# Linear attention and MLP on one Trainium2 core: w_out as whole rows, stepped weight loads, and a new order of the start

## Chip, cores and metric

The kernel runs on 1 core of one Trainium2 chip. The metric is device microseconds (us) of the run; the median of a kernel's runs is quoted. A profiled execution's own length is called its span. Ratios between kernels are the mean time of one kernel's runs over that of the other's of the same rounds, so they are not quite the ratio of the medians quoted beside them; brackets hold the 95% interval. A verdict of faster or slower asks for 2%: by that rule the changed kernel and a_v2 below are slower, a_packed, a_tiles, b_rows and a_best are unclear, and the rest are the same as before; where a smaller difference is called a gain or a loss, its interval excludes 1.

In the lines of the profile PE is TensorE and PEld its weight loads, ACT ScalarE, DVE VectorE, POOL GpSimd and SP the sync engine; a q marks an engine's sequencer, which issues DMAs, and L585 is a line of kernel.py. `ps` is a PSUM bank, `xT` the transposed x, `gT` the product that the second layer reads, `cosh` the cosine, `sp` the decay's logarithm but for its sign (the `f` line before it is the exponential that it needs), `vb` v in bf16, and `qkt` the transposed q and k. The granted clock is the share of TensorE's full clock that the profile shows as granted.

## The reference

Linear attention with a decay per channel (4 batches, 8 heads, 768 tokens, head size 48), and then an MLP on its 3072 tokens of 384 values:

```python
f = 1.0 / (1.0 + np.exp(-f_logit))
for t in range(S):
    state = f[:, :, t, :, None] * state + np.einsum('bhd,bhe->bhde', k[:, :, t], v[:, :, t])
    y[:, :, t] = np.einsum('bhd,bhde->bhe', q[:, :, t], state)
# ... x = y as (3072, 384)
h = x @ w_in              # 384 x 2048
g = h * np.cos(h)
return g @ w_out          # 2048 x 384
```

## The kernel before

Attention works on 24 chunks of 128 tokens. Each chunk loads f, k, q and v. The decay sums of f go through TensorE (L416, L419), the states and scores follow, and the chunk's y is transposed to x. The MLP takes units of 128 or 256 tokens: a first-layer matmul group fills one PSUM bank (`ph`), ScalarE takes its cosine, VectorE multiplies, and the second layer sums 16 products to a 128x384 tile.

A list scheduler in Python (`Plan`) puts every operation on an engine and in an order when the kernel is built, from estimated durations and a table of priorities. Each engine then runs its list strictly in order. The framework adds the semaphores: it makes the reader wait for the transfer that wrote what it reads.

```python
GATES = [1, 0, 0, 0, 2, 3, 2, 2]      # four w_in slices, four w_out slices: each issued after
                                      # the v of this chunk has been used
QUEUES = ["SAAA", "ASSA", "SSSS", ...]  # who issues f, k, q, v of a chunk: S sync, A ScalarE, P GpSimd
QK_DMA = [7, 10, 13, ...]             # chunks whose q, k are transposed by DMA instead of TensorE
X_DMA = [11, 13, 15, ...]             # the same for y

w_in_bf = cpool.tile([128, KM, d_ff], BF16, name="w_in_bf")       # one tile, written by four DMAs
w_in_v = [Val(ap=w_in_bf[:, :, i * 512:(i + 1) * 512]) for i in range(NW)]

def load_weights(part, i, prio):
    if part == 0:
        dst = w_in_v[i]
        src = moe_w_in.rearrange("(km p) f -> p km f", p=128)[:, :, i * 512:(i + 1) * 512]
    else:
        dst = w_out_v[i]
        src = moe_w_out.rearrange("(kf p) m -> p kf m", p=128)[:, i * 4:(i + 1) * 4, :]
    # ... nc.gpsimd.dma_start(out=dst.ap, in_=src), gated by GATES

# first layer, one PSUM bank:
def g1(e, j=j, ph=ph):
    for g in range(G):
        f0 = (j * G + g) * 128
        for m in range(KM):
            nc.tensor.matmul(ph.ap[:, g * T:(g + 1) * T],
                             lhsT=w_in_bf[:, m, f0:f0 + 128], rhs=x[:, m, :], start=..., stop=...)
# P.op(..., reads=xs + [w_in_v[j * G // 4]])  then cosine on ScalarE, product on VectorE

order = P.run()
with tc.manual_schedule():
    table = None
    for o in order:
        if o.table is not None:
            if o.table == "E" and table != "E":
                nc.scalar.preload_act_table_set("natural_log_exp_and_others")
            table = o.table
        o.fn(o.eng)
```

Of the kernel before, what the change touches and what calls it, by code (L numbers as in the profile page):

```python
# [96 lines left out]
class Plan:  # L97


    SEM = 70.0  # L100
    DMA = 1.092
    WAIT = {'PE': 0.0, 'POOL': 97, 'DVE': 154, 'ACT': 409}
    RING = 3500.0
# [37 lines left out]
    def run(self):  # L141
# [15 lines left out]
        while len(order) < n:  # L157
            picks, first = [], {}
            for o in ready:
# [18 lines left out]
                for e, cost in o.eng.items():  # L178
# [3 lines left out]
                    if o.dma and e == "SP":  # L182
                        s = max(s, ring[0] - self.RING)
# [66 lines left out]
def kernel(  # L250
# [12 lines left out]
    C = 128  # L263
# [10 lines left out]
    GROUPS = [1, 1, 1, 1, 1, 1, 2, 2, 2, 2, 1, 1, 3, 2, 3]  # L274
    UNITS = [128, 128, 128, 128, 256, 256, 256, 256, 128, 128, 256, 256, 256, 256, 128, 128]
    ATT = [-10.16, -8.17, -4.99, 0.11, 6.14, 3.09, 4.17, 1.33, 2.29, 1.86, 5.6, 0.47, 2.61, 2.34, -2.58, -2.8, -5.5, -1.05, -1.76, -4.41, -2.39, 0.76, 4.74, -4.25]
    DEC = [-0.66, -1.41, 2.39, -0.73, 3.32, 1.22, -3.35, 0.65, -0.34, -1.28, 0.8, 2.4, 1.16, 2.8, -2.87, -1.43, -4.69, -4.08, -1.68, -2.98, 3.95, -1.37, -1.73, -0.08]
    MM1 = [6.38, -2.33, 5.15, 0.82, -3.52, 2.06, 3.26, -6.82, -3.23, -5.74, -4.4, -6.91, -6.01, -9.31, -13.24, -5.93, -9.36, -13.7, -5.96, -13.1, -8.32, -22.13, -16.43, -24.95]
    MM2 = [8.02, 8.08, 14.32, 8.13, 9.49, 9.01, 11.35, 24.51, 13.52, 4.27, 10.31, 19.31, 13.3, 8.66, 22.93, -2.07, -3.64, 10.08, 13.04, -1.99, 17.19, -1.14, 7.0, 16.95]

    GATES = [1, 0, 0, 0, 2, 3, 2, 2]

    QUEUES = ["SAAA", "ASSA", "SSSS", "SSSS", "SSSS", "SSSS", "SSSS"]

    QK_DMA = [7, 10, 13, 14, 15, 17, 18, 19, 20, 21, 22, 23]
    X_DMA = [11, 13, 15, 18, 19, 20, 22, 23]
    FAST = 12
    GT_BUFS = {128: 4, 256: 4}
# [22 lines left out]
    nld = 6  # L311
# [4 lines left out]
    vbS = slots("vb", 4, [128, H, D])  # L316
    spS = slots("sp", 5, [128, H, 64], zero=272.0)
    bS = slots("b", 4, [128, H * D + NP], F32)
    biS = slots("bi", 3, [128, H * D], F32)
    qkS = slots("qk", 4, [128, 2 * NP * C], zero=470.0)  # L320
    qktS = slots("qkt", 4, [128, 2 * NP, C])
    amS = slots("am", 4, [128, 4, C])
    szS = slots("sz", 3, [128, NP, 2 * D], zero=200.0)
    yS = slots("y", 3, [128, d_model])
    stS = slots("st", 2, [128, NP, D], F32)
    x_sb = [cpool.tile([128, KM, TOK], BF16, name=f"xT_{i}") for i in range(NT)]
    gS = {T: slots(f"gT{T}", n, [128, KF, T]) for T, n in GT_BUFS.items()}
    coS = slots("cosh", 4, [128, TOK])
    otS = slots("ot", 4, [128, d_model], F32)
    base = banks("ps", 8)  # L330
    moe_cap = [5, 0]
    phS = Banks(base, "ph", 4, [moe_cap])
    poS = Banks(base, "po", 2, [moe_cap])
    paS = Banks(base, "pa", 2)
    miS = Banks(base, "mi", 4)
# [8 lines left out]
    P.op({"POOL": 1100.0}, masks, prio=-1.0)  # L344
# [11 lines left out]
# [3 lines that stand above are left out]
            src = moe_w_in.rearrange("(km p) f -> p km f", p=128)[:, :, i * 512:(i + 1) * 512]  # L359
        else:  # L360
            dst = w_out_v[i]
            src = moe_w_out.rearrange("(kf p) m -> p kf m", p=128)[:, i * 4:(i + 1) * 4, :]
        o = P.op({"POOL": 850.0}, lambda e, dst=dst, src=src: nc.gpsimd.dma_start(
            out=dst.ap, in_=src), writes=[dst], prio=prio, lat=2200.0, dma=2400.0 if part == 0 else 2200.0)
# [15 lines left out]
    def chunk_load(b, c, prio):  # L380
        vals = []
        for pool, src in ((fS, f_logit), (kS, k), (qS, q), (vS, v)):
# [6 lines left out]
                 writes=[t], prio=prio, lat=3000.0 if way == "P" else 2000.0, dma=980.0)  # L389
# [3 lines left out]
    def decay_group(chunks, g, prio):  # L393
# [18 lines left out]
        for (b, c, ld, sp) in outs:  # L412
# [10 lines left out]
            P.op({"PE": 365.0}, pe, reads=[sp], writes=[pc], prio=prio, lat=170.0)  # L423
# [202 lines left out]
    for g, size in enumerate(GROUPS):  # L626
# [3 lines left out]
        for j, item in enumerate(decay_group(grp, g, n + DEC[g])):  # L630
            attend(*item, prio=n + j + ATT[n + j])
            if n + j == 0:
                for i in range(NW):
                    load_weights(0, i, 0.2 + 0.1 * i)
# [46 lines left out]
```

## Time and profile before

| | before |
|---|---|
| median of 3 runs | 192.81 us (192.74 to 194.06) |
| span of the profiled run (its time was 194.2 us) | 192.4 us |
| PE busy | 170.5 us, 89% |
| work PE cannot avoid (counts times spacing) | 160 us |
| PE's loss: whole, and before 50 us | 32.7 and 24.8 us |

"Loss" is time in which PE does not do work that it must do: the span, or a stretch of it, less the sum of its matmuls, each at the spacing that it has in a packed run. It counts waits, and also matmuls that run at half rate. The prediction shows how the spacings were read.

For comparing with later kernels, two stretches. First PE in the timeline of the kernel before (start, duration, engine, line, operation, output and inputs, count):

```profile
19.63 1.46 PE L585 MATMUL ps<-xT,w_in_bf 128*128 128x128 bf16 x12
...
22.61 0.83 PE L585 MATMUL ps<-xT,w_in_bf 128*128 128x128 bf16 x12
```

The first group of twelve first-layer matmuls runs at 19.63, the second at 22.61. The first takes 1.46 us for twelve, the second 0.83: the same instructions, at half rate and at full rate. Then the weight loads of the first layer by themselves (shortest, median and longest in ns):

```profile
L585 PEld LDWEIGHTS <-w_in_bf x768: 95/98/152, 19.6 to 180.7; 128*128 128x128 bf16 x192
```

### The profile page before, as it was taken

How to read it: one execution, taken by the hardware profiler on the slowest of the kernel's cores; microseconds unless marked ns; L12 is line 12 of the kernel's file. 1: busy time of each engine (PE TensorE's matmuls, PEld its weight loads, DVE VectorE, ACT ScalarE, POOL GpSimd, SP SyncE). 2: the span in 40 equal slices, each digit the busy share in tenths (PEclk: the TensorE clock that was granted, in tenths of full speed). 3: DMA queues.
4: the chain of work that ended last, by engine and by line, in shares of the span. 5: the costliest groups of instructions: out<-in, count | busy, mean ns of one | idle time of the engine just before them, and what ended most of it. 6: DMA issues, size and time to landing. Idle time of an engine off the chain costs nothing.

```text
span 192.4 us, 5056 instructions
## 1 busy us (share of the span) xinstructions
PE 170.5 (89%) x1960; PEld 129.5 (67%) x1960; DVE 138.0 (72%) x259; ACT 137.4 (71%) x250; POOL 65.6 (34%) x105
## 2 busy tenths in 40 slices
PE   0056996879999999999999999999999999999992
PEld 0035786747679668767769887588686785788861
DVE  6057995667978999995988798269878369782900
ACT  0434788599289968998989769998369992473620
POOL 5250806240030076029167211598321491200000
PEclk9999997899999999999999999999999999999999
DMA  6999999998995999996399899799993383102022
GB/s 137 218 205 191 217 186 154 197 200 157 200 232 126 221 189 217 197 258 113 85 271 121 180 200 219 179 224 166 201 243 111 117 120 87 54 0 82 3 84 81
DMA packets 123032, 31.00 MB, mean 161 GB/s; under 512 B 116352, under 2 KB 123008, under 8 KB 123008
## 3 DMA queue, kind: packets, MB, share of 16 engines
q1 hardware_dynamic: 114096, 26.55, 68.9%
q0 software_dynamic: 3712, 3.15, 10.4%
q10 hardware_dynamic: 5200, 0.98, 3.1%
q8 instruction: 15, 0.25, 0.6%
q14 instruction: 9, 0.07, 0.1%
HBM read 25.17 MB, written 4.72 MB: 155 GB/s over the span
## 4 chain that ended last, share of the span: by engine, by line
PE 78%; DVE 8%; ACT 3%; issue 3%; ACTq 3%; DMA 2%; DVEq 0%
PE ps L585 33%; PE ps L606 29%; PE ps L489 4%; PE ps L470 3%; ACTq L388 3%; DVE qk L447 3%; PE ps L540 2%; DVE am L496 2%; PE ps L416 2%; PE ps L508 2%; DMA out_dram<-ot 2%; PE ps L561 1%; PE ps L543 1%; DVE st L523 1%; ACT L648 1%
## 5 line engine op out<-in xcount | busy, mean ns | idle before, releaser
L606 PE MATMUL ps<-w_out_bf,gT 128*128 128x384 bf16 x384 | 70.6, 326 | 0.0
L585 PE MATMUL ps<-xT,w_in_bf 128*128 128x128 bf16 (+1 forms) x768 | 69.5, 251 | 0.6 <-DVE xT L550 0.4
L596 DVE TENSOR_TENSOR gT<-ps,cosh 128x512 bf16<-128x512 f32 x96 | 60.5, 686 | 11.0 <-ACT cosh L592 10.7
L585 PEld LDWEIGHTS <-w_in_bf 128*128 128x128 bf16 x768 | 60.9, 100 | 6.6 <-issue 0.9
L592 ACT ACTIVATE cosh<-ps 128x512 bf16<-128x512 f32 x96 | 53.6, 604 | 9.5 <-PE ps L585 6.8
L606 PEld LDWEIGHTS <-gT 128*128 128x128 bf16 x384 | 34.5, 97 | 19.3
L496 DVE TENSOR_TENSOR am<-ps,umask 128x512 bf16<-128x512 f32 x48 | 31.2, 685 | 4.0 <-PE ps L489 3.6
L527 POOL TENSOR_TENSOR sz<-st,b 64x192 bf16<-64x192 f32 x32 | 16.1, 503 | 52.0 <-DVE st L523 39.0
L452 POOL CAST vb<-v 128x384 bf16<-128x384 f32 x24 | 13.0, 543 | 27.4 <-DMA v<-in_v_dram 16.6
L447 POOL TENSOR_TENSOR qk<-k,bi 128x384 bf16<-128x384 f32 x16 | 16.0, 1003 | 7.5 <-ACT bi L426 7.3
L615 ACT COPY ot<-ps 128x384 f32<-128x384 f32 x13 | 6.2, 484 | 15.5 <-PE ps L606 15.5
L447 POOL TENSOR_TENSOR qk<-q,b 128x384 bf16<-128x384 f32 x13 | 13.0, 1001 | 12.0 <-ACT b L426 8.7
L416 PE MATMUL ps<-sp,umask 128*128 128x384 bf16 x24 | 8.4, 349 | 9.5 <-ACT sp L404 9.4
L648 ACT ACT_TABLE_LOAD x9 | 11.5, 1283 | 7.1 <-issue 7.0
L550 ACT CAST y<-ps 128x384 bf16<-128x384 f32 x19 | 9.0, 482 | 10.4 <-PE ps L543 4.8
L426 ACT ACTIVATE b<-ps 128x388 f32<-128x388 f32 x24 | 11.9, 494 | 5.5 <-PE ps L419 4.3
L523 DVE TENSOR_TENSOR st<-ps,sz 64x192 f32<-64x192 f32 x32 | 11.3, 352 | 4.1 <-PE ps L508 3.2
L476 DVE COPY qkt<-ps 128x512 bf16<-128x512 bf16 x21 | 8.4, 420 | 7.7 <-PE ps L470 7.6
L470 PE MATMUL ps<-ident,qk 128*128 128x128 bf16 x96 | 9.3, 238 | 4.6 <-DVE qk L447 4.5
L447 DVE TENSOR_TENSOR qk<-q,b 128x384 bf16<-128x384 f32 x11 | 8.1, 740 | 7.1 <-ACT b L426 7.0
L404 ACT ACTIVATE sp<-f 128x384 bf16<-128x384 f32 x24 | 12.6, 523 | 0.7
L419 PEld LDWEIGHTS <-sp 128*128 128x128 bf16 x96 | 6.2, 100 | 10.1 <-issue 8.1
(38 smaller groups left out, 152.2 us busy)
## 6 DMA issues: line engine op xcount, KB each, us to landing
out_dram<-ot SPq DMA_DIRECT2D x24, 192.0 KB, 2.9
f<-in_f_logit_dram SPq DMA_DIRECT2D x23, 192.0 KB, 3.7
k<-in_k_dram SPq DMA_DIRECT2D x23, 192.0 KB, 4.0
q<-in_q_dram SPq DMA_DIRECT2D x23, 192.0 KB, 4.0
v<-in_v_dram SPq DMA_DIRECT2D x22, 192.0 KB, 3.9
w_in_bf<-in_moe_w_in_dram POOLq DMA_DIRECT2D x4, 384.0 KB, 7.8
w_out_bf<-in_moe_w_out_dram POOLq DMA_DIRECT2D x4, 384.0 KB, 7.0
v<-in_v_dram ACTq DMA_DIRECT2D x2, 192.0 KB, 6.5
```

Of the source, the lines that this page charges most:

```text
L404: nc.scalar.activation(out=sp.ap[:, :, 0:D], in_=f.ap, func=AF.Ln, bias=1.0)
L447: lambda e, src=src, w=w, dst=dst: E(e).tensor_mul(out=dst.ap, in0=src.ap, in1=w.ap[:, 0:H * D].rearrange("p (h d) -> p h d", d=D)),
L452: o = P.op({"POOL": 510.0}, lambda e: nc.gpsimd.tensor_copy(out=vf.ap, in_=v32.ap), reads=[v32], writes=[vf], prio=prio)
L470: nc.tensor.transpose(out=o[:, i, :], in_=qk.ap[:, j * C:(j + 1) * C], identity=ident)
L496: nc.vector.tensor_mul(out=am.ap, in0=pa.ap.rearrange("p (a n) -> p a n", n=C), in1=umask[:, None, :].broadcast_to([128, 4, C]))
L523: P.op({"DVE": 370.0}, lambda e, g=g, sg=sg: nc.vector.tensor_add(out=sg.ap, in0=psv(g), in1=block(S_in.ap, g)), reads=[ps, S_in], writes= ...
L527: o = P.op(cost, lambda e, g=g, srcap=srcap, out=out: E(e).tensor_mul(out=out.ap, in0=srcap(), in1=bt.ap[rows(g), H * D:, None].broadcast_ ...
L585: nc.tensor.matmul(ph.ap[:, g * T:(g + 1) * T], lhsT=w_in_bf[:, m, f0:f0 + 128], rhs=x[:, m, :], start=(g == 0 and m == 0), stop=(g == G - ...
L592: P.op({"ACT": 490.0}, lambda e, ph=ph, co=co: nc.scalar.activation(out=co.ap, in_=ph.ap, func=AF.Sin, bias=HALF_PI), reads=[ph], writes=[ ...
L596: P.op({"DVE": 605.0}, lambda e, ph=ph, co=co, gv=gv: nc.vector.tensor_mul(out=gv.ap, in0=ph.ap.rearrange("p (g t) -> p g t", t=T), in1=co ...
L606: nc.tensor.matmul(po.ap[:, 0:d_model], lhsT=gT.ap[:, j, i * 128:(i + 1) * 128], rhs=w_out_bf[:, j, :], start=(j == 0), stop=(j == KF - 1))
L648: nc.scalar.preload_act_table_set("natural_log_exp_and_others")
```

## The change

Its intent: read w_out from memory in longer pieces (four whole rows to a partition, 6 KB), begin the exponentials sooner, start w_out's loads sooner, take work from PE by DMA transposes, and give the scheduler more buffers and better constants. A row of w_out in a partition is now row 4p + j of its slice, so row p of the first layer's output must be the same one. Therefore the weight loads read w_in with a step of four columns. Core of the diff (the new priority tables, groups, costs and buffer counts are cut; so is a loop of dummy matmuls, which runs zero times):

```diff
-    UNITS = [128, 128, 128, 128, 256, 256, 256, 256, 128, 128, 256, 256, 256, 256, 128, 128]
+    UNITS = [128, 128, 128, 128, 256, 128, 128, 128, 128, 256, 128, 128, 256, 256, 128, 128, 256, 256]
-    GATES = [1, 0, 0, 0, 2, 3, 2, 2]
+    GATES = [1, 1, 0, 1, 1, 2, 2, 1]
-    QUEUES = ["SAAA", "ASSA", "SSSS", "SSSS", "SSSS", "SSSS", "SSSS"]
+    QUEUES = ["SAAP", "SSSS", "SSSA", "SSSS", "SSSS", "SSAA", "SSSS"]
-    QK_DMA = [7, 10, 13, 14, 15, 17, 18, 19, 20, 21, 22, 23]
-    X_DMA = [11, 13, 15, 18, 19, 20, 22, 23]
+    QK_DMA = [7, 10, 12, 13, 14, 15, 16, 17, 18, 19, 20, 21, 22, 23]
+    X_DMA = [7, 8, 11, 12, 13, 14, 16, 18, 19, 20, 21, 22, 23]
+    WARM = 0
-    gS = {T: slots(f"gT{T}", n, [128, KF, T]) for T, n in GT_BUFS.items()}
+    gS = slots("gT", BUFS["g"], [128, KF, 256])
...
-            src = moe_w_out.rearrange("(kf p) m -> p kf m", p=128)[:, i * 4:(i + 1) * 4, :]
+            src = moe_w_out[i * 512:(i + 1) * 512, :].rearrange("(p j) m -> p j m", j=4)
...
-                    f0 = (j * G + g) * 128
+                    s0, f0 = divmod(j * G + g, 4)
                     for m in range(KM):
                         nc.tensor.matmul(ph.ap[:, g * T:(g + 1) * T],
-                                         lhsT=w_in_bf[:, m, f0:f0 + 128], rhs=x[:, m, :],
+                                         lhsT=w_in_bf[:, m, s0 * 512 + f0:(s0 + 1) * 512:4],
+                                         rhs=x[:, m, :],
...
+                P.op({"ACT": 1300.0}, lambda e: nc.scalar.preload_act_table_set(
+                    "natural_log_exp_and_others"), prio=0.0)
...
-        table = None
+        table = "E"
```

More of the change, by code (lines that the diff above doesn't have):

```diff
@@ L97 @@
 class Plan:
-    SEM = 70.0
-    DMA = 1.092
-    WAIT = {'PE': 0.0, 'POOL': 97, 'DVE': 154, 'ACT': 409}
-    RING = 3500.0
+    SEM = 80.0
+    DMA = 1.074
+    WAIT = {'PE': 0.0, 'ACT': 441.0, 'DVE': 176.0, 'POOL': 368.0}
+    RING = 2600.0
     def __init__(self):
@@ L181, in run @@
                     s = max(at, free[e])
-                    if o.dma and e == "SP":
+                    if o.dma and e != "POOL":
                         s = max(s, ring[0] - self.RING)
@@ L271 @@
     NT = n_tokens // TOK
-    GROUPS = [1, 1, 1, 1, 1, 1, 2, 2, 2, 2, 1, 1, 3, 2, 3]
-    UNITS = [128, 128, 128, 128, 256, 256, 256, 256, 128, 128, 256, 256, 256, 256, 128, 128]
-    ATT = [-10.16, -8.17, -4.99, 0.11, 6.14, 3.09, 4.17, 1.33, 2.29, 1.86, 5.6, 0.47, 2.61, 2.34, -2.58, -2.8, -5.5, -1.05, -1.76, -4.41, -2.39, 0.76, 4.74, -4.25]
-    DEC = [-0.66, -1.41, 2.39, -0.73, 3.32, 1.22, -3.35, 0.65, -0.34, -1.28, 0.8, 2.4, 1.16, 2.8, -2.87, -1.43, -4.69, -4.08, -1.68, -2.98, 3.95, -1.37, -1.73, -0.08]
@@ L278 @@
-    MM1 = [6.38, -2.33, 5.15, 0.82, -3.52, 2.06, 3.26, -6.82, -3.23, -5.74, -4.4, -6.91, -6.01, -9.31, -13.24, -5.93, -9.36, -13.7, -5.96, -13.1, -8.32, -22.13, -16.43, -24.95]
-    MM2 = [8.02, 8.08, 14.32, 8.13, 9.49, 9.01, 11.35, 24.51, 13.52, 4.27, 10.31, 19.31, 13.3, 8.66, 22.93, -2.07, -3.64, 10.08, 13.04, -1.99, 17.19, -1.14, 7.0, 16.95]
-    GATES = [1, 0, 0, 0, 2, 3, 2, 2]
-    QUEUES = ["SAAA", "ASSA", "SSSS", "SSSS", "SSSS", "SSSS", "SSSS"]
-    QK_DMA = [7, 10, 13, 14, 15, 17, 18, 19, 20, 21, 22, 23]
@@ L286 @@
-    X_DMA = [11, 13, 15, 18, 19, 20, 22, 23]
-    FAST = 12
-    GT_BUFS = {128: 4, 256: 4}
+    GROUPS = [1, 1, 1, 1, 1, 1, 1, 1, 2, 2, 1, 1, 2, 3, 3, 1, 1]
+    UNITS = [128, 128, 128, 128, 256, 128, 128, 128, 128, 256, 128, 128, 256, 256, 128, 128, 256, 256]
+    ATT = [19.22, 11.51, -4.12, -47.95, -0.79, -26.21, 1.62, -77.63, -4.72, -35.67, 4.42, -7.77, -2.18, -5.67, -30.35, -11.85, -82.53, -43.97, -72.33, -27.9, 14.06, -10.62, -90.56, -29.09]
+    DEC = [0.76, -37.4, -9.67, 3.24, -28.16, -26.29, -29.09, -13.37, -2.77, -22.73, -5.51, -16.89, -9.11, -15.8, -5.52, -15.87, -14.6, -47.95, -13.31, -46.04, 12.51, -38.96, -48.3, 2.6]
@@ new lines @@
+    MM1 = [31.51, -33.43, 5.49, -61.55, -31.58, -28.33, -84.44, -57.9, -92.94, -33.48, -15.49, -110.01, -86.82, -88.64, -49.22, -3.19, -33.68, 38.91, -19.02, -27.86, -47.17, -40.28, -25.45, -2.63]
+    MM2 = [17.68, 38.21, -7.69, 15.13, 1.62, -48.95, 20.6, 14.96, 12.07, -1.71, 12.39, 6.86, 48.36, 89.6, 44.19, 59.19, 89.52, -38.97, 26.19, 0.43, -54.56, -74.55, -67.19, 15.11]
+    GATES = [1, 1, 0, 1, 1, 2, 2, 1]
+    QUEUES = ["SAAP", "SSSS", "SSSA", "SSSS", "SSSS", "SSAA", "SSSS"]
+    QK_DMA = [7, 10, 12, 13, 14, 15, 16, 17, 18, 19, 20, 21, 22, 23]
@@ L290 @@
+    X_DMA = [7, 8, 11, 12, 13, 14, 16, 18, 19, 20, 21, 22, 23]
+    FAST = 10
+    WARM = 0
+    BUFS = {"ld": 7, "vb": 6, "sp": 6, "b": 6, "bi": 4, "qk": 5, "qkt": 6, "am": 6, "sz": 4, "y": 4, "st": 2, "co": 5, "ot": 5, "g": 6}
+    CAPS = [6, 4, 3, 3, 3]
     cpool = ctx.enter_context(tc.tile_pool(name="const", bufs=1))
@@ L309, in banks @@
         return Slots([ppool.tile([128, 512], F32, name=f"{name}_{i}") for i in range(n)], name)
-    nld = 6
+    nld = BUFS["ld"]
     fS = slots("f", nld, [128, H, D], F32)
@@ L315 @@
     vS = slots("v", nld, [128, H, D], F32)
-    vbS = slots("vb", 4, [128, H, D])
-    spS = slots("sp", 5, [128, H, 64], zero=272.0)
-    bS = slots("b", 4, [128, H * D + NP], F32)
-    biS = slots("bi", 3, [128, H * D], F32)
-    qkS = slots("qk", 4, [128, 2 * NP * C], zero=470.0)
-    qktS = slots("qkt", 4, [128, 2 * NP, C])
-    amS = slots("am", 4, [128, 4, C])
-    szS = slots("sz", 3, [128, NP, 2 * D], zero=200.0)
-    yS = slots("y", 3, [128, d_model])
-    stS = slots("st", 2, [128, NP, D], F32)
+    vbS = slots("vb", BUFS["vb"], [128, H, D])
+    spS = slots("sp", BUFS["sp"], [128, H, 64], zero=272.0)
+    bS = slots("b", BUFS["b"], [128, H * D + NP], F32)
+    biS = slots("bi", BUFS["bi"], [128, H * D], F32)
+    qkS = slots("qk", BUFS["qk"], [128, 2 * NP * C], zero=470.0)
+    qktS = slots("qkt", BUFS["qkt"], [128, 2 * NP, C])
+    amS = slots("am", BUFS["am"], [128, 4, C])
+    szS = slots("sz", BUFS["sz"], [128, NP, 2 * D], zero=200.0)
+    yS = slots("y", BUFS["y"], [128, d_model])
+    stS = slots("st", BUFS["st"], [128, NP, D], F32)
     x_sb = [cpool.tile([128, KM, TOK], BF16, name=f"xT_{i}") for i in range(NT)]
-    gS = {T: slots(f"gT{T}", n, [128, KF, T]) for T, n in GT_BUFS.items()}
-    coS = slots("cosh", 4, [128, TOK])
-    otS = slots("ot", 4, [128, d_model], F32)
+    gS = slots("gT", BUFS["g"], [128, KF, 256])
+    coS = slots("cosh", BUFS["co"], [128, TOK])
+    otS = slots("ot", BUFS["ot"], [128, d_model], F32)
     base = banks("ps", 8)
-    moe_cap = [5, 0]
-    phS = Banks(base, "ph", 4, [moe_cap])
-    poS = Banks(base, "po", 2, [moe_cap])
-    paS = Banks(base, "pa", 2)
-    miS = Banks(base, "mi", 4)
+    moe_cap = [CAPS[0], 0]
+    phS = Banks(base, "ph", CAPS[1], [moe_cap])
+    poS = Banks(base, "po", CAPS[2], [moe_cap])
+    paS = Banks(base, "pa", CAPS[3])
+    miS = Banks(base, "mi", CAPS[4])
     w_in_bf = cpool.tile([128, KM, d_ff], BF16, name="w_in_bf")
@@ L343, in masks, with idle @@
         make_upper_triangular(nc, umask, val=1.0, diag=True)
-    P.op({"POOL": 1100.0}, masks, prio=-1.0)
+    mk = Val()
+    P.op({"POOL": 1100.0}, masks, writes=[mk], prio=-1.0)
+    warm = Val(phS)
+    for i in range(WARM):
+        def idle(e):
+            for _ in range(2):
+                nc.tensor.matmul(warm.ap[:, 0:128], lhsT=ident, rhs=ident, start=True, stop=True)
+        P.op({"PE": 220.0 if i < 16 else 112.0}, idle, reads=[mk], writes=[warm], prio=1e6)
     for pool, cost in zeroed:
@@ L361, in load_weights @@
             dst = w_out_v[i]
-            src = moe_w_out.rearrange("(kf p) m -> p kf m", p=128)[:, i * 4:(i + 1) * 4, :]
+            src = moe_w_out[i * 512:(i + 1) * 512, :].rearrange("(p j) m -> p j m", j=4)
         o = P.op({"POOL": 850.0}, lambda e, dst=dst, src=src: nc.gpsimd.dma_start(
-            out=dst.ap, in_=src), writes=[dst], prio=prio, lat=2200.0, dma=2400.0 if part == 0 else 2200.0)
+            out=dst.ap, in_=src), writes=[dst], prio=prio, lat=3000.0, dma=2350.0 if part == 0 else 2000.0)
         gate(o, GATES[part * NW + i])
@@ L388, in chunk_load @@
             P.op(eng, lambda e, t=t, ap=ap, dma=dma: dma.dma_start(out=t.ap, in_=ap),
-                 writes=[t], prio=prio, lat=3000.0 if way == "P" else 2000.0, dma=980.0)
+                 writes=[t], prio=prio, lat=3000.0 if way == "P" else 1250.0, dma=980.0)
             vals.append(t)
@@ L421, in pe @@
                                      rhs=umask[:, C - 1:C], start=False, stop=(p == NP - 1))
-            P.op({"PE": 365.0}, pe, reads=[sp], writes=[pc], prio=prio, lat=170.0)
+            P.op({"PE": 268.0}, pe, reads=[sp], writes=[pc], prio=prio, lat=170.0)
             def ex(e, pc=pc, o=bt, s=-1.0, n=H * D + NP):
@@ L480, in attend @@
             P.op({"SP": 1000.0}, lambda e: nc.sync.dma_start_transpose(out=qkt.ap, in_=qk.ap),
-                 reads=[qtd, ktd], writes=[qdt, kdt], prio=prio, lat=2000.0, dma=1400.0)
+                 reads=[qtd, ktd], writes=[qdt, kdt], prio=prio, lat=1250.0, dma=1400.0)
         pas, ams = [Val(paS), Val(paS)], [Val(amS), Val(amS)]
@@ L492, in pe @@
                                      start=(p == 0), stop=(p == NP - 1))
-        P.op({"PE": 330.0}, pe, reads=[kdt, qdt], writes=pas, prio=prio, lat=170.0)
+        P.op({"PE": 420.0}, pe, reads=[kdt, qdt], writes=pas, prio=prio, lat=170.0)
         for pa, am in zip(pas, ams):
@@ L567, in attend @@
             P.op({"SP": 700.0}, lambda e: nc.sync.dma_start_transpose(out=x.ap, in_=yt.ap),
-                 reads=[yt], writes=[x], prio=prio, lat=2000.0, dma=480.0)
+                 reads=[yt], writes=[x], prio=prio, lat=1250.0, dma=480.0)
     def moe(u, t0, T):
         n0 = t0 // C
-        xs, gT = xT[n0:(t0 + T) // C], Val(gS[T])
+        xs, gT = xT[n0:(t0 + T) // C], Val(gS)
         x = x_sb[t0 // TOK][:, :, t0 % TOK:t0 % TOK + T]
```

## The prediction

> **What bounds the kernel now.** I began with the page's slices: TensorE (PE) and the DMA engines side by side.
>
> ```profile
> PE   0056996879999999999999999999999999999992
> ...
> DMA  6999999998995999996399899799993383102022
> ```
>
> A slice is 4.8 us. From the eleventh on PE is full to the end; before it PE has holes, and the DMA row is full there. So there are two regimes. The table of windows shows their border (PE busy with its count of matmuls, then PEld, DVE, ACT, POOL, granted clock, mean DMA share, GB/s):
>
> ```profile
> 0.00:10.00 10.00, 0.56 (x5) 0.41 (x5) 2.96 (x8) 2.35 (x4) 4.53 (x15) 1.00 1.07 179
> 10.00:20.00 10.00, 6.36 (x65) 4.43 (x66) 6.90 (x16) 4.81 (x11) 3.00 (x6) 1.00 1.26 196
> 20.00:30.00 10.00, 8.13 (x142) 7.47 (x139) 9.74 (x18) 8.03 (x13) 4.31 (x7) 1.00 1.24 201
> 30.00:40.00 10.00, 8.85 (x107) 7.33 (x108) 6.17 (x13) 7.40 (x13) 3.33 (x6) 0.83 1.13 183
> 40.00:50.00 10.00, 8.79 (x103) 6.39 (x102) 7.37 (x13) 8.56 (x14) 2.79 (x4) 1.00 0.88 173
> 50.00:180.00 130.00, 129.00 (x1483) 98.03 (x1482) 102.52 (x191) 102.87 (x193) 47.60 (x70) 1.00 0.78 161
> ```
>
> Busy time alone flatters PE, since a matmul waiting for its neighbour's end counts as busy. For what PE must do I used its spacing in packed runs, which the chain that ended last shows near the end (start, duration, what):
>
> ```profile
> 165.76 5.24 PE ps L585 x48
> ...
> 175.65 5.36 PE ps L585 x96
> 181.01 7.82 PE ps L606 x48
> ```
>
> That is 109 ns for a first-layer matmul with 256 tokens, 55.8 ns with 128 tokens, 163 ns for a second-layer one (384 columns). With the counts of the groups: 384 x 0.109 = 41.9, 384 x 0.0558 = 21.4, 384 x 0.163 = 62.6. The attention's matmuls in the same way (transposes 56 ns, scores 42, state and output 42 and 25, decay sums about 0.27 us a chunk) make about 34. Sum 160 us; the span is 192.4. So **32 us are lost by PE**. Summing the same per-instruction costs in 10 us stretches: 25 us are lost before 50 us, 4 between 50 and 180, the rest in the tail (last PE work ends at 188.8, then a 0.48 us copy and the last output's landing). The middle is as good as done; only the first 50 us, the tail, or PE's own work can pay.
>
> The start of the chain says what the first 8 us are:
>
> ```profile
> 0.74 0.48 ACTq L388
> ...
> 1.25 0.74 ACTq L388
> ...
> 2.02 1.19 ACTq L388
> ...
> 3.24 1.65 ACTq L388
> ...
> 4.93 2.00 ACTq L388
> ...
> 6.96 0.09 ACT L648
> 7.04 1.21 issue
> 8.25 0.53 ACT f L401
> ```
>
> ScalarE (ACT) issues five loads, each slower than the last, then loads its table, then starts the first exponential at 8.25. In the trace the first f tile landed at 4.16 us, so **4 us of that wait are ACT's own**. After it the landings rule: single loads arrive 0.9 us apart up to 12.7 us, the four slices of w_in at 15.1, 17.5, 20.0 and 22.7, of w_out at 28.2, 31.0, 36.0 and 39.8, and the sixth chunk is in at 47.6. PE cannot do its first-layer work before 22.7, nor finish a second-layer tile before 39.8.
>
> **What the skill says.** (1) "DMA: Bandwidth & Descriptors", section "Issuing engines are not separate DMA queues": loads started by different engines share the same 16 DMA engines, and spreading them saves only issue time. The trace agrees with the sharing: whichever queue issued them, the loads land 0.9 us apart. But issue time is not small here: the fifth issue held ACT for 2.00 us. (2) The same page, "Specifications", gives 512 bytes as the least for full rate. The loads have rows of 192 bytes: 192 KB in 0.9 us is 0.22 MB/us. A w_in slice reads 2 KB rows, 0.79 MB in 2.5 us, 0.31 MB/us. w_out's rows are 1536 bytes already, so joining four to 6144 gains little. (3) "SBUF — State Buffer", section "SBUF: two separate sides", box on cachelines: two accesses to each 16-byte line are enough for full rate, so a step of up to 8 bf16 is called free by its list; the same text's two hits per line would mean 8 bytes, 4 bf16. (4) "TensorE: Matmul & The Clock Gate", section "Weight-path perf modes", lists column steps up to 1,024 as allowed for fast weight loads, "packed or strided". Nothing in the kernel before loads weights with a step, so no run yet shows (3) or (4).
>
> **The change part by part.**
>
> *w_out as four whole rows.* To match it, h's rows are permuted, and the first layer's weight loads read w_in with a step of four elements (8 bytes). The number of loads follows the units: 12 of 128 tokens and 6 of 256, against 8 and 8, so 18 x 48 = 864 for 768. If stepped loads stay hidden, first-layer PE time is 576 x 0.0558 + 288 x 0.109 = 63.5 us against 63.3: nothing. DMA: w_out now 7 us to landing, 4 x about 0.2 us saved at w_in's rate: under 1 us, in the start where DMA counts.
>
> *First table load and queues.* The order of instructions shows ACT issuing k and q of chunk 0, then the table load, then the exponential; f goes on the sync queue, v by GpSimd. ACT is free at 2.0, the table at 3.3, f lands at about 4.2. Chunk 0's exponential moves from 8.25 to about 4.3: **4 us on the chain's start**. But w_in ends the stretch, not chunk 0. Its first slice is issued after v of chunk 0 (about 8 us, as now), the other three after v of chunk 1 (9.9 to 12.4, now 9.6 to 13.9). Landings of about 14.5 to 22 against 15.1 to 22.7: **about 1 us**, plus 1 us because attention of chunks 0 to 2 is then already out of the way.
>
> *w_out earlier.* Two slices follow w_in at once, in place of loads for chunk 3. PE may begin second-layer work near 26 us, now 35.3. It is the same DMA work in another order, so I credit **1 us** for filling.
>
> *More DMA transposes.* 14 of qk for 12, 13 of x for 8. PE loses 2 x 8 transposes x 56 ns = 0.9 and 5 x 3 x 63 ns = 0.95: **1.8 us less PE work** where PE is full. DVE and ACT lose about nine evacuations of some 0.4 us, which is off the path. DMA gains about 5 us, where its share is 0.78.
>
> *One pool of gT, more buffers, bank caps 6/4/3/3/3.* Six tiles of 256 tokens take the room of the old two pools. A little of the 4 us lost in the middle: **0.3 us**. *No dummy matmuls*: the loop runs zero times and the kernel before had none: 0. Table loads stay 18 in all.
>
> Sum: 1 + 1 + 1 + 1.8 + 0.3 = 5.1 us less. I take off 0.3 for small new waits of a rearranged order: 192.8 - 4.8 = **188.0 us**.
>
> **The rivals.** *A: the step spoils the weight loads.* If a stepped load cannot hide behind a 128-token matmul and the pair takes the 100 ns that one load lasts in the trace, that is 576 x 44 ns = 25 us: about 213. Half that harm would be 200. For it: no measurement. Against it: 8 bytes still give two hits a line, and the author re-measured other PE costs in his plan but left this one. I give it 8%.
>
> *B: the early DMA wall stays.* Weights and six chunks are the same bytes, and DMA is full until 43 us. Then earlier exponentials and the new order merely shift waits, and only the transposes pay: about 191. For it: DMA's full slices. Against it: PE work per chunk with both layers is 6.7 us for 3.6 us of loads, so which bytes come first does matter. This is the likeliest miss, 35%.
>
> *C: the new order is much better planned*, its constants being nearer to what landings show: most of the 8 us lost from 23 to 50 us vanish, about 184. 15%.
>
> **Range and chances.** 2% below is 189.0. The central case and C fall below it, B between, A above. Low 184.5, high 193.0. Faster 0.55, same 0.36, slower 0.09.
>
> **What would show it.** Right: the first exponential near 4.3 us; last w_in slice landing near 22; first second-layer matmul before 30; first-layer matmuls with 128 tokens still 56 ns apart in packed runs; 80 PE transposes of qk and 33 of y; PE loss before 50 us about 21 or 22 us, in the middle still about 4. Wrong: spacing above 60 ns (A); PE loss before 50 us still near 25 (B), or below 18 (C); new holes in the middle from later x tiles.

## More of the kernel before

Kernels sent together share the runs of the kernel before.

The profiled run of the kernel before was 1.4 us slower than its median, so its loss is, if anything, too large beside that of later kernels.

## The result

The changed kernel takes **200.53 us** (median of 4 runs, 198.60 to 203.56, one of them slow), against 192.91 before in its rounds (4 runs): ratio 1.035 [1.026, 1.044], slower by 3.5%. Executions over 1.5% slower than the fastest of the same kernel are left out of the means. 188.0 was predicted, with a range to 193.0.

| us | before | after |
|---|---|---|
| span | 192.4 | 198.2 |
| work PE cannot avoid | 159.8 | 158.3 |
| PE's loss, whole | 32.7 | 39.9 |
| ... before 50 us | 24.8 | 30.0 |
| ... 50 to 180 us | 4.1 | 5.6 |
| first exponential | 8.25 | 4.05 |
| last w_in slice landed | 22.7 | 23.0 |
| first second-layer matmul | 35.3 | 33.5 |
| w_out slices landed | 28.2, 31.0, 36.0, 39.8 | 25.1, 27.1, 43.3, 46.8 |

PE's work fell by 1.5 us (1.8 were planned); its loss rose by 7.2, of which 5.2 fall before 50 us. The slices of the page after, in tenths, show where:

```profile
PE   0571489499998999999999999999999799999991
...
DMA  7999999982299497999999998999899946503003
```

A slice is 4.95 us. PE begins better (5, 7) but has a 1 and a 4 at 15 to 25 us and another 4 at 35 us. In the DMA row the full stretch ends sooner, and then there are two slices with a 2: transfers that could have run weren't issued (the sync engine issues none from 37.4 to 53.6 us, while it stands before its first store of an output). In the table of windows the loss is in the same places (columns as in the prediction):

```profile
0.00:10.00 10.00, 2.90 (x29) 2.00 (x30) 6.36 (x16) 4.13 (x7) 5.13 (x16) 1.00 1.04 181
10.00:20.00 10.00, 4.64 (x53) 3.26 (x51) 5.60 (x13) 5.42 (x10) 5.01 (x8) 1.00 1.20 193
20.00:30.00 10.00, 6.43 (x59) 5.62 (x60) 3.56 (x7) 1.38 (x3) 0.00 (x0) 1.00 1.04 194
30.00:40.00 10.00, 7.06 (x93) 6.04 (x92) 5.96 (x11) 7.09 (x12) 2.17 (x4) 0.88 1.13 210
40.00:50.00 10.00, 9.93 (x121) 8.08 (x119) 7.06 (x15) 7.54 (x12) 2.75 (x5) 0.78 0.52 94
50.00:180.00 130.00, 127.83 (x1582) 100.73 (x1580) 101.47 (x188) 105.44 (x195) 49.67 (x73) 1.00 0.89 171
```

Between 20 and 30 us PE issued 59 matmuls, where before it issued 142, and ScalarE, VectorE and GpSimd had little to do either (1.38, 3.56 and 0.00 us). All wait for something that lies before them. PE's timeline names it (in brackets: idle time before, and what ended it):

```profile
15.28 0.49 PE L554 MATMUL ps<-sz,qkt 128*128 128x96 bf16 x4
20.73 0.27 PE L597 MATMUL ps<-xT,w_in_bf 128*128 128x128 bf16 x1 [4.95 <-DMA w_in_bf<-in_moe_w_in_dram]
23.05 1.36 PE L597 MATMUL ps<-xT,w_in_bf 128*128 128x128 bf16 x11 [2.06 <-DMA w_in_bf<-in_moe_w_in_dram]
...
28.31 5.34 PE L597 MATMUL ps<-xT,w_in_bf 128*128 128x128 bf16 x72
33.49 1.46 PE L619 MATMUL ps<-w_out_bf,gT 128*128 128x384 bf16 x8
36.72 0.32 PE L427 MATMUL ps<-sp,umask 128*128 128x384 bf16 x1 [1.77 <-ACT sp L415]
```

**First hole.** PE is through with its attention at 15.8 and has first-layer work next. The first slice of w_in is there at 15.1. Yet the first matmul runs at 20.73, alone, and the other eleven of its group at 23.05. In the trace the four slices landed at 15.13, 18.07, 20.59 and 23.00. So the first matmul went with the third landing, the second with the fourth. One matmul reads one slice only; it waited for all of them.

The built program says why. Its listing of waits, in PE's order, for the first-layer weight loads that wait for a DMA (one DMASW is one weight or v load by GpSimd, in their order of issue):

```
before: 133 L585 Ldweights w_in_bf [waits DMASW0]
        203 L585 Ldweights w_in_bf [waits DMASW1]
        291 L585 Ldweights w_in_bf [waits DMASW2]
        339 L585 Ldweights w_in_bf [waits DMASW3]
after:  157 L597 Ldweights w_in_bf [waits DMASW3,DMASW2,DMASW1]
        159 L597 Ldweights w_in_bf [waits DMASW4]
```

Before, the first load waited for one slice, and the next slice was first asked for 70 instructions on. Now the first two loads ask for all four. A contiguous piece of 128 columns is seen to lie in one slice; the stepped piece, it seems, is not.

**Second hole.** The chain that ended last goes through a load of chunk 2, whose f, k and q had landed by 15.6 us (start, duration, what):

```profile
11.95 11.06 DMA w_in_bf<-in_moe_w_in_dram
...
32.35 4.68 DMA v<-in_v_dram
```

This is v of chunk 2. It stands in ScalarE's own list, behind six cosines of the first layer:

```profile
24.45 0.60 ACT L605 ACTIVATE cosh<-ps 128x512 bf16<-128x512 f32 x1 [6.86 <-PE ps L597]
...
31.01 1.94 ACT L605 ACTIVATE cosh<-ps 128x512 bf16<-128x512 f32 x3 [0.59 <-PE ps L597]
32.35 0.37 ACTq L399 DMA_DIRECT2D v<-in_v_dram  x1
```

ScalarE waited 6.86 us for PE's late first layer, and only then got to issue v. v landed at 37.03; and the third and fourth w_out slices are gated on it, as GpSimd's timeline shows:

```profile
37.16 0.51 POOL L463 CAST vb<-v 128x384 bf16<-128x384 f32 x1 [20.45 <-DMA v<-in_v_dram]
37.62 0.59 POOL L374 DMA_DIRECT2D w_out_bf<-in_moe_w_out_dram  x1
...
40.66 0.59 POOL L374 DMA_DIRECT2D w_out_bf<-in_moe_w_out_dram  x1
```

GpSimd sat 20.45 us, and these two slices landed 7.3 and 7.0 us later than before. No wait of PE for them is recorded, though: PE's list has only eight second-layer matmuls at this place (at 33.49), in a_tiles_v2 below too. Of this hole PE itself shows 1.77 us for ScalarE and then 0.59 us for `vb` of chunk 2.

**What went as meant.** The table load stands at 2.02, the first exponential at 4.05:

```profile
2.02 1.28 ACT L646 ACT_TABLE_LOAD   x1 [2.02 <-issue]
4.05 0.52 ACT L412 ACTIVATE f<-f 128x384 f32<-128x384 f32 x1 [0.75 <-DMA f<-in_f_logit_dram]
```

And stepped weight loads last longer, yet stay hidden:

```profile
L597 PEld LDWEIGHTS <-w_in_bf x864: 111/113/152, 20.7 to 189.1; 128*128 128x128 bf16 x173
```

The median load takes 113 ns for 98, but first-layer matmuls with 256 tokens still come 109 ns apart near the end (30 in 3.27 us and 18 in 1.97; one run of 48 took 5.36, 112 each). Groups of twelve with 128 tokens take 0.67 us, 56 ns each.

### The profile page after: what moved, and what is told of

The parts are those of the page before. It is cut to its first block, busy times and chain, and to the rows that moved or that the text cites. A ratio compares the mean times of both kernels' runs of the same rounds, so it can differ in the third digit from the quotient of the medians.

```text
span 198.2 us, 5168 instructions
## 1 busy us (share of the span) xinstructions
PE 172.8 (87%) x2025; PEld 136.0 (69%) x2025; DVE 135.3 (68%) x255; ACT 137.7 (69%) x249; POOL 64.7 (33%) x105
## 4 chain that ended last, share of the span: by engine, by line
PE 67%; DMA 15%; DVE 7%; POOL 3%; ACT 3%; issue 2%; SPq 2%; ACTq 0%; POOLq 0%
PE ps L597 29%; PE ps L619 26%; DMA v<-in_v_dram 7%; DMA w_in_bf<-in_moe_w_in_dram 6%; PE ps L500 3%; DMA qkt<-qk 3%; PE ps L551 2%; DVE gT L609 2%; DVE am L507 2%; PE ps L481 2%; DVE qk L458 2%; SPq L399 2%; PE ps L554 2%; PE ps L427 2%; PE ps L519 1%
## 5 line engine op out<-in xcount | busy, mean ns | idle before, releaser
L597 PE MATMUL ps<-xT,w_in_bf 128*128 128x128 bf16 (+1 forms) x864 | 71.8, 244 | 7.0 <-DMA w_in_bf<-in_moe_w_in_dram 7.0
L597 PEld LDWEIGHTS <-w_in_bf 128*128 128x128 bf16 x864 | 67.5, 116 | 9.3 <-issue 5.3
L605 ACT ACTIVATE cosh<-ps 128x512 bf16<-128x512 f32 x96 | 54.6, 604 | 24.6 <-PE ps L597 20.2
L463 POOL CAST vb<-v 128x384 bf16<-128x384 f32 x24 | 12.1, 506 | 54.2 <-DMA v<-in_v_dram 45.7
L458 POOL TENSOR_TENSOR qk<-q,b 128x384 bf16<-128x384 f32 x14 | 14.1, 1006 | 5.5 <-ACT b L437 3.2
L458 POOL TENSOR_TENSOR qk<-k,bi 128x384 bf16<-128x384 f32 x14 | 14.1, 1006 | 0.2
L487 DVE COPY qkt<-ps 128x512 bf16<-128x512 bf16 x16 | 6.6, 421 | 10.7 <-PE ps L481 10.6
L412 ACT ACTIVATE f<-f 128x384 f32<-128x384 f32 x24 | 12.5, 522 | 0.8 <-DMA f<-in_f_logit_dram 0.7
L500 PE MATMUL ps<-qkt 48*128 48x128 bf16 x192 | 10.4, 233 | 1.8 <-DMA qkt<-qk 1.3
L437 ACT ACTIVATE bi<-ps 128x384 f32<-128x384 f32 x24 | 11.9, 495 | 0.0
L605 ACT ACT_TABLE_LOAD x9 | 11.5, 1283 | 0.2
```

The lines of the kernel that those rows point to most:

```text
L412: nc.scalar.activation(out=f.ap, in_=f.ap, func=AF.Exp, scale=-1.0)
L437: nc.scalar.activation(out=o.ap, in_=pc.ap[:, 0:n], func=AF.Exp, scale=s)
L458: lambda e, src=src, w=w, dst=dst: E(e).tensor_mul(out=dst.ap, in0=src.ap, in1=w.ap[:, 0:H * D].rearrange("p (h d) -> p h d", d=D)),
L500: nc.tensor.matmul(pas[g].ap[:, p * C:(p + 1) * C], lhsT=kdt.ap[64 * g:64 * g + D, p, :], rhs=qdt.ap[64 * g:64 * g + D, p, :], start=(p == ...
L597: nc.tensor.matmul(ph.ap[:, g * T:(g + 1) * T], lhsT=w_in_bf[:, m, s0 * 512 + f0:(s0 + 1) * 512:4], rhs=x[:, m, :], start=(g == 0 and m == 0),
L605: P.op({"ACT": 490.0}, lambda e, ph=ph, co=co: nc.scalar.activation(out=co.ap, in_=ph.ap, func=AF.Sin, bias=HALF_PI), reads=[ph], writes=[ ...
```

## Experiments

**Theory.** Two waits made the start worse: the dependency of stepped reads on all four slices (S), and v of chunk 2 behind cosines on ScalarE (V). **Rivals.** R1: the stepped read or the new layout of w_out is itself slow. R2: the new order is worse at large, with many small waits, and mending these two gives little. R3: PE's half rate in the start (twelve matmuls in 1.46 us against 0.83) is the real cost. In all experiments the order of every engine stayed that of the kernel edited, apart from the moves told. All results were correct. The expectations name the theories in their own way: their W is S (with V as a second, smaller cost), their Rival S is R1, O is R2, M is S and V in series, C is R3, D says that landings set the start, and F that the landing of f of chunk 3 does.

One more rival needs no run of its own: a lower granted clock. It was 0.93 over the first 50 us of the changed kernel and 0.97 before; but it is 0.93 in a_tiles_v2 as well, which has none of the loss.

### 1. a_packed: the changed kernel with the old layout and packed weight loads

```diff
-            src = moe_w_out[i * 512:(i + 1) * 512, :].rearrange("(p j) m -> p j m", j=4)
+            src = moe_w_out.rearrange("(kf p) m -> p kf m", p=128)[:, i * 4:(i + 1) * 4, :]
-                                         lhsT=w_in_bf[:, m, s0 * 512 + f0:(s0 + 1) * 512:4],
+                                         lhsT=w_in_bf[:, m, (4 * s0 + f0) * 128:(4 * s0 + f0 + 1) * 128],
```

> The changed kernel with w_in read in packed columns and w_out in its old layout, every engine's order kept. Theory W (the stepped weight loads carry a coarse dependency: in the changed kernel the first first-layer load waits for three w_in slices and the second for the fourth, so PE sits from 15.8 to 23.05 us and starts again at half clock): each operation waits for its own slice again, the first first-layer matmul starts at 15.8 us, the span falls by 6 to 8 us, to about 193 us. Rival O (the new order and w_out right behind w_in are at fault, the wait for w_in hides slack): 198 us or more, the same PE hole moving to chunk 2's v. Rival S (a stepped load is slow in itself): faster too, but a_tiles is not.

Measured: four runs, 197.15 and 198.94 fast, 200.26 slow, and 294.89 in the profiled one, at a granted clock of 0.587. Ratio to before 1.0235 [1.016, 1.031], where the changed kernel had 1.035. About 193 us was expected: a miss. Undoing layout and step together gives back about 1.1%, so most of the loss remains. Alone it does not separate S from R1. The slow run's profile can still be read in the start, where PE runs as in the later kernels up to 21 us: the first hole is gone (first-layer work at 15.49), and ScalarE now stands before the issue of v of chunk 2, until an unrelated load has landed:

```profile
31.05 0.43 ACTq L399 DMA_DIRECT2D v<-in_v_dram  x1
31.58 1.09 ACT L605 ACTIVATE cosh<-ps 128x512 bf16<-128x512 f32 x2 [5.16 <-DMA k<-in_k_dram]
```

The next experiment has the same wait.

### 2. a_tiles: stepped loads kept, w_in in four tiles

```diff
-    w_in_bf = cpool.tile([128, KM, d_ff], BF16, name="w_in_bf")
+    w_in_t = [cpool.tile([128, KM, 512], BF16, name=f"w_in_{i}") for i in range(d_ff // 512)]
-    w_in_v = [Val(ap=w_in_bf[:, :, i * 512:(i + 1) * 512]) for i in range(NW)]
+    w_in_v = [Val(ap=w_in_t[i][:, :, :]) for i in range(NW)]
-                                         lhsT=w_in_bf[:, m, s0 * 512 + f0:(s0 + 1) * 512:4],
+                                         lhsT=w_in_t[s0][:, m, f0:512:4],
```

The read is the same, the dependency can only be on its own slice. The listing of waits has DMASW1, 2, 3 and 4 again, one each, at rows 157, 243, 291 and 339.

> The changed kernel with w_in in four tiles, one to a slice: steps and whole rows of w_out kept, so only the dependency becomes exact. Theory W: the same as a_packed within 1 us, about 193 us, first first-layer matmul at 15.8 us. Rival S: stays near 200 us while a_packed is faster. Rival O: 198 us or more, as a_packed.

Measured: 197.83 us (197.36 to 198.57), ratio 1.0227 [1.018, 1.027]: the same as packed loads, though not the 193 that was expected. So the step and the layout show no cost by themselves (against R1; b_tiles below is the cleaner test), and the first hole is the dependency. PE's timeline:

```profile
16.75 1.48 PE L597 MATMUL ps<-xT,w_in 128*128 128x128 bf16 x12
...
26.39 1.46 PE L619 MATMUL ps<-w_out_bf,gT 128*128 128x384 bf16 x8 [0.65 <-DMA w_out_bf<-in_moe_w_out_dram]
35.14 0.48 PE L427 MATMUL ps<-sp,umask 128*128 128x384 bf16 x1 [7.29 <-ACT sp L415]
```

The first layer now begins at 16.75 instead of 20.73, and the second at 26.39 instead of 33.49. But what PE won it waits away at once: 7.29 us for ScalarE. ScalarE's timeline:

```profile
22.02 2.61 ACT L605 ACTIVATE cosh<-ps 128x512 bf16<-128x512 f32 x4 [0.53 <-PE ps L597]
31.06 0.45 ACTq L399 DMA_DIRECT2D v<-in_v_dram  x1
31.62 1.08 ACT L605 ACTIVATE cosh<-ps 128x512 bf16<-128x512 f32 x2 [6.99 <-DMA k<-in_k_dram]
```

ScalarE had reached the issue of v at 24.6 and stood there until 31.06. The release was the landing of k of chunk 4, at 31.04, a load with which v has nothing to do. The built program has a wait on that issue, too (`v_2 DMACopy [waits DMAHW7]`; DMAHW0 in the changed kernel): the loads of the sync engine and of ScalarE share eight semaphores in rotation, and an issue waits until the load that used its semaphore last has landed. So v's wait has two forms: behind late cosines, or behind an unrelated load.

### 3. a_v2: v of chunk 2 to the sync queue, behind q of chunk 2

```diff
     order = P.run()
+    o, at = loads[2, 3], loads[2, 2]          # v and q of chunk 2
+    order.remove(o)
+    order.insert(order.index(at) + 1, o)
+    o.eng = "SP"                              # issued by nc.sync.dma_start
```

> The changed kernel with one load moved: v of chunk 2 from ScalarE's queue, where it was issued at 32.35 us behind six cosines, to the sync queue behind q of chunk 2. Theory W: this is a second, smaller cost; PE's hole from 15.8 to 23.05 stays, vb of chunk 2 is made before 25 us in place of 37.2, the third and fourth w_out slices land before 40 us in place of 43.3 and 46.8; 1 to 3 us less, about 198.5 us. Rival O: this is the main cost: 5 us or more less, 195 us or below.

Measured: 199.05 us (198.08 to 199.27), ratio 1.0277 [1.023, 1.033]. The first hole is still there, 5.32 and 2.07 us. Alone it is worth 1.5 us (200.53 less 199.05, from different calls; the intervals of the two ratios overlap, so this is not clear of noise). The two repairs alone look small, which at this point would have spoken for R2.

### 4. b_rows: the kernel before, with only the whole rows and the stepped loads

```diff
-            src = moe_w_out.rearrange("(kf p) m -> p kf m", p=128)[:, i * 4:(i + 1) * 4, :]
+            src = moe_w_out[i * 512:(i + 1) * 512, :].rearrange("(p j) m -> p j m", j=4)
-                    f0 = (j * G + g) * 128
+                    s0, f0 = divmod(j * G + g, 4)
-                                         lhsT=w_in_bf[:, m, f0:f0 + 128], rhs=x[:, m, :],
+                                         lhsT=w_in_bf[:, m, s0 * 512 + f0:(s0 + 1) * 512:4], rhs=x[:, m, :],
```

> The kernel before with only the whole rows of w_out and the stepped w_in loads; order kept. Theory W: its first first-layer matmul, which ran at 19.63 us with two slices landed, now waits for the last slice at about 22.6; 1 to 3 us more, about 195 us, while the packed-run spacing at 128 tokens stays 56 ns. Rival S: 128-token spacing above 60 ns and 5 us or more. If neither: within 0.5 us of before.

Measured: 196.40 us (195.91 to 198.48) against 193.32, ratio 1.0171 [1.011, 1.024]. One part of the change, put into the old kernel, costs 3.1 us. Its timeline has the same pattern, one matmul and then a wait:

```profile
20.53 0.27 PE L585 MATMUL ps<-xT,w_in_bf 128*128 128x128 bf16 x1 [0.78 <-DMA w_in_bf<-in_moe_w_in_dram]
23.02 1.34 PE L585 MATMUL ps<-xT,w_in_bf 128*128 128x128 bf16 x11 [2.23 <-DMA w_in_bf<-in_moe_w_in_dram]
```

### 5. a_tiles_v2: both repairs, edits 2 and 3 together

> The changed kernel with both edits: four w_in tiles, and v of chunk 2 on the sync queue. Theory M (two costs in series, each hides the other: with exact dependencies alone, ScalarE reached the issue of v of chunk 2 at 24.6 us and was held there until 31.06 us by the load that had its DMA semaphore before, which gave PE a new hole of 7.3 us): together the new hole shrinks to 2 us or less, chunk 3's exponential starts near 28 us, and 4 to 7 us more are saved than by the tiles alone (197.8): 191 to 194 us, level with before. Rival O (the order of loads, w_out right behind w_in, starves chunk 3 and later chunks): only 0 to 2 us more, 196 us or above, PE waiting for landings of chunk 3's tiles.

Measured: **192.25 us** (191.76 to 192.65), ratio 0.994 [0.990, 0.998].

| | us | gained on the changed kernel |
|---|---|---|
| changed kernel | 200.5 | |
| tiles alone | 197.8 | 2.7 |
| v alone | 199.1 | 1.5 |
| both | 192.3 | 8.3 |

Together they give twice the sum of the two. The waits lie one behind the other: with the first gone PE reaches the second sooner and waits longer there (7.29 us for 1.77), and with only the second gone the first still stands. PE's loss falls to 32.0 us, of which 23.5 before 50 us; that of the kernel before is 32.7 and 24.8. So theory S + V holds, and R2 falls: the order, without its two waits, is as good as the one before and a little better, by 0.6%, with 1.5 us less work for PE in it.

```profile
21.16 5.67 PE L597 MATMUL ps<-xT,w_in 128*128 128x128 bf16 x72
...
29.91 0.32 PE L427 MATMUL ps<-sp,umask 128*128 128x384 bf16 x1 [1.77 <-ACT sp L415]
```

The 7.29 us are 1.77 now. But 72 matmuls need 5.67 us here, 79 ns each for the 56 of full rate: what is left of R3.

### 6. a_tiles_act: also q and v of chunk 5 off ScalarE

The edit is the same as 3, for loads (5, q) and (5, v), behind k and q of chunk 5.

> As a_tiles_v2, with q and v of chunk 5 also moved from ScalarE's to the sync queue, behind k of chunk 5. Theory M: another 0 to 2 us, from the wait for v of chunk 5 near 50 us; 190 to 193 us. Rival O: no further change.

Measured: 192.88 us (192.18 to 195.01), ratio 0.9999 [0.992, 1.008]. No gain over 192.25 shows, within the 0.8% of the interval. This fits that not each load on ScalarE does harm, only one that other work hangs on.

### 7. b_tiles: the kernel before with whole rows, stepped loads and four tiles

The edits of 4 and 2 together.

> The kernel before with whole rows and stepped loads as in b_rows, but four w_in tiles. If the coarse dependency is all that the layout costs: level with before within 0.5 us (b_rows was 1.7% slower), first first-layer matmul at 19.6 us. If whole rows save DMA time in the start as I had predicted: up to 1 us faster. If stepped loads cost in themselves: stays 1% or more slower.

Measured: 193.10 us (192.97 to 193.34) against 193.11, ratio 0.9986 [0.995, 1.002]. With the dependency gone the layout neither costs nor gains, within 0.5%. This settles R1, and also says that the longer rows of w_out save nothing visible; I had put them at under 1 us.

### 8. b_head: the kernel before with f and v of chunk 1 off ScalarE's queue

```diff
     order = P.run()
+    # f of chunk 1 to the sync queue behind f of chunk 0, v of chunk 1 behind q of chunk 1
```

With three issues instead of five before its table load, ScalarE starts its first exponential early, in the old order.

> The kernel before with f and v of chunk 1 moved from ScalarE's to the sync queue, so that its first table load is done near 4.5 us and not 8.25. My prediction gave the change's early table load 2 us in all (1 through earlier w_in slices, 1 through attention being out of the way): then 191 us. If the start is bound by the DMA engines and the w_in slices, 0 to 0.7 us: 192.5 us or above, PE waiting longer for the first slice.

Measured: the table load at 3.29 and the first exponential at 4.59 instead of 8.25, and 193.12 us (191.31 to 193.94), ratio 0.9973 [0.990, 1.004]. The 3.7 us at the very start of the chain are worth nothing that three rounds can tell. The move has a second side, however: in its trace the w_in slices landed 1.2 to 1.5 us later than before (the last at 24.17), so the run gives the worth of the moved loads, not of an early exponential alone.

### 9 to 11. a_warm_head, a_warm_late, a_warm: dummy matmuls against the half rate

All on top of a_tiles_v2. Dummy matmuls on a spare PSUM bank are to keep PE busy: 44, 14, 6 and 12 of them before 20 us (head), or 28, 10, 12 and 10 between about 27 and 34 us (late), or both.

```diff
+    def dummies(n):
+        for _ in range(n):
+            nc.tensor.matmul(base.aps[7][:, 0:128], lhsT=ident, rhs=ident, start=True, stop=True)
# called in PE's order at the start and after its operations 0, 2, 16 (head); 27, 30, 31, 32 (late)
```

> a_tiles_v2 with 76 dummy 128-column matmuls in PE's empty time before 20 us (44 before the first decay sum, 14, 6 and 12 later), into a PSUM bank not in use. Theory C (what is left of the start is partly PE at half rate: in a_tiles_v2 128-column matmuls come 107 ns apart up to about 25 us, 56 ns later): the 72 first-layer matmuls that took 5.67 us take about 4.0 us or end with the last slice at about 24.5 us, and 0.5 to 1.5 us are saved: about 191.2 us. Rival D (slices and landings set the start): below 0.3 us, or slower because dummies delay attention.

Measured: 193.84 us (192.66 to 194.77), ratio 1.0017 [0.999, 1.005]: a miss. The 72 first-layer matmuls were done sooner, by 24.5 us, but ScalarE's next exponential, that of chunk 3, was not, and PE waited 3.93 us for it:

```profile
29.27 0.52 ACT L412 ACTIVATE f<-f 128x384 f32<-128x384 f32 x1 [2.89 <-DMA f<-in_f_logit_dram]
```

f of chunk 3 landed at 29.25 (28.40 in a_tiles_v2). In this trace v of chunk 2 landed at 21.11 (there 25.73), so the w_out slice that waits for it was issued at 21.69 (there 26.30) and landed at 28.99, just before f. That the slice took the DMA engines from f fits, but is not shown, and the dummies need not be its cause: a_warm_late, which has none before 27 us, also has v at 19.40, the slice at 20.09 and f at 29.34. Single executions differ by this much, so why this run gained nothing stays open.

> a_tiles_v2 with 60 dummy matmuls between 28 and 34 us only (28, 10, 12, 10), where PE waits for ScalarE and VectorE and falls back to 107 ns. Theory C: PE keeps 56 ns from 28 to 40 us; the operations from 31 to 39 us end 2 to 3 us earlier; 1 to 3 us saved: about 190.5 us. Rival D: below 0.3 us, since chunk 4's landings set that stretch.

Measured: 192.93 us (191.76 to 194.52), ratio 0.9981 [0.994, 1.002]. Nothing. Yet the dummies did what they were to do: from 30 to 40 us the granted clock reads 1.00, where it reads 0.66 in a_tiles_v2.

> Both sets of dummies. Theory C: 2 to 4 us saved over a_tiles_v2 (192.25), about 189.5 us, over 1% faster than the kernel before. Rival D: within 0.5 us of a_tiles_v2.

Measured: 191.49 us (189.72 to 194.23, one slow), ratio 0.9868 [0.983, 0.991]. In this one f of chunk 3 landed at 27.70. The gain on a_tiles_v2 (0.994) is 0.7%, less than the 2 to 4 us that were expected, so R3 is at most a small part of the loss by itself.

### 12. a_best: both sets of dummies, and the fourth w_out slice after the third

```diff
+    order.remove(weights[1, 3])
+    order.insert(order.index(weights[1, 2]) + 1, weights[1, 3])
```

Slices are counted by their place in w_out here. Also 36 first dummies instead of 44. In a_tiles_v2 the fourth slice is one of the two that GpSimd issues early, from 12.8 us on; now it is issued last, at about 32, so that the DMA engines are free for the loads of chunks 2 and 3.

> a_warm with 36 in place of 44 dummies ahead of the first decay sum, and the w_out slice that stood second behind w_in (the fourth slice, not needed before 40 us) sent last of the four. Theory F (with PE kept at full rate the start waits for f of chunk 3, which landed at 27.7 us in a_warm behind w_in and two w_out slices): f of chunk 3 lands 1.5 to 2.5 us sooner, near 25.7 us, and 0.5 to 2 us are saved over a_warm: about 190 us, 1.5 to 2% faster than the kernel before. If the total of the bytes sets the start and not their order: within 0.5 us of a_warm (191.5).

Measured: **188.94 us** (188.50 to 190.18, 6 runs), ratio 0.9775 [0.973, 0.982]: 2.25% faster than the kernel before (1.8 to 2.7%), and 5.8% than the changed one (188.94 for 200.53, from different calls). f of chunk 3 landed at 25.52. PE's timeline:

```profile
20.20 2.87 PE L599 MATMUL ps<-xT,w_in 128*128 128x128 bf16 x48
...
28.34 0.33 PE L429 MATMUL ps<-sp,umask 128*128 128x384 bf16 x1
```

The first 48 take 60 ns each, the wait for ScalarE at 28.34 is gone. How much of the last step comes from the slice's place and how much from eight dummies fewer was not taken apart; that f lands sooner is what was expected of the slice's place (near 25.7).

## Why the prediction was wrong

By its own steps:

1. **Head of the chain, about 4.3 us: right** (4.05). **Spacing of 56 ns, 80 and 33 transposes, PE work less by 1.8 us: right** (80, 33; the work fell by 1.5 us).
2. **"If stepped loads stay hidden, first-layer PE time is 63.5 us against 63.3: nothing." The first step that failed.** They stay hidden (113 ns, still 56 ns apart). But I asked only how fast such a load is, also in rival A, and not what it waits for. As compiled it waits for all four slices. Alone, in the old order, that costs 3.1 us (b_rows), with tiles nothing (b_tiles). The listing of waits that I show above could have been read before predicting; I read the order only.
3. **"Landings of about 14.5 to 22 ... about 1 us, plus 1 us because attention is then already out of the way": wrong.** The last slice landed at 23.0, and an early first exponential brought nothing visible in the old kernel (b_head, 0.9973 [0.990, 1.004], with the w_in slices later there). This is what rival B said of the DMA wall.
4. **"w_out earlier: PE may begin second-layer work near 26, 1 us": the second step that failed.** Two slices did land by 27.1, but PE came at 33.5, and two slices landed 7 us later than before. I read that f, k, q and v of chunk 2 were spread over queues, but not that v's issue stands in ScalarE's list behind six cosines and has a wait of its own, nor that two w_out slices are gated on that v. With both waits gone PE does begin it at 26.67 (a_tiles_v2), but only eight such matmuls stand there.
5. **"I take off 0.3 for small new waits": mis-sized.** The new waits, those of steps 2 and 4 together, were 8.3 us (changed kernel less a_tiles_v2); step 2 alone gives 2.7 of it back, step 4 alone 1.5.
6. **Longer rows of w_out, under 1 us:** not seen (b_tiles 0.9986).

With both waits gone the rest of the change gives 0.6% (a_tiles_v2), about 1.1 us. This is near the 191 of rival B: of my sum of 5.1 us there remains no more than the transposes' 1.5 us of PE work; that it is the transposes, no run here shows. My "what would show it" was good for finding the fault: loss before 50 us of 30, where 21 to 22 was to be right and near 25 rival B, lies outside of all the cases that I had named. I had no rival in which the wait for weights got worse.

Packed loads gain no more than stepped ones in tiles with the new order, since both run into the second wait (5.16 us of ScalarE in a_packed, 6.99 in a_tiles). Left open: what the extra 1.5 us of loss after 50 us in the changed kernel are made of. They are nearly gone in a_tiles_v2 (4.3 us against 5.6), so they seem to follow from the start.

## What to carry to other kernels

A change of how an operand is addressed is also a change of what it depends on: after any new step, view or tile shape, list the semaphores that the first readers wait for, and give each separately loaded piece its own tile. A DMA issue in a computing engine's list waits behind that engine's work, and for an unrelated earlier load; keep a load off that list if other work hangs on it. Two waits in series hide each other, so judge repairs together before dropping either, and look at which transfers stand ahead of the load that is needed next: with one w_out slice sent last (and eight dummies fewer) f of chunk 3 landed at 25.52 instead of 27.70.

## What the Trainium skill lacked or had wrong

- "TensorE: Matmul & The Clock Gate", section "Back-to-back issue gap", gives about 81 ns a matmul as the sustained spacing of load and matmul pairs with 128 columns. Here pairs ran 56 ns apart (96 in 5.36 us before, 12 in 0.67 us with stepped loads). The page's 106.7 ns cold and 55.6 ns warm (section "Wait — 56ns, not 53.3ns?") agree with the two rates seen (12 in 1.28 us and in 0.67 us from one group's start to the next). The granted clock of the views shows this difference only in part: in the changed kernel it reads 0.50 from 37.57 to 44.40 us, where twelve take 1.28 us, but 1.00 from 20 to 30 us, where twelve take 1.28 us as well; its trace holds no record of the clock before 30.75 us.
- The same page, section "Weight-path perf modes", allows stepped weight loads and gives no time. They took 113 ns for 98 with a step of 8 bytes, hidden at a spacing of 56 ns.
- "DMA: Bandwidth & Descriptors", section "Issuing engines are not separate DMA queues", calls the issuing time usually small beside the transfer. In the kernel before an issue held ScalarE for 2.00 of the 6.9 us from issue to landing. In a_tiles it held ScalarE for 6.4 us (24.6 to 31.06), with the wait for another load's landing.
- No page has it that stepped reads of one tile that several DMAs write wait for all of these: 3.1 us in b_rows, none with a tile to each DMA.
- "ScalarE: Activation LUTs", section "What ACT_TABLE_LOAD costs", gives 1283 ns and about 1380 ns of drain. The load lasted 1.28 us, and in a_tiles the exponential at 34.02 began 0.02 us after it ended (32.72 + 1.28), and the load 0.02 us after the cosine before it: no drain is seen.
